# Lower parts of the first layer's weight units: computed by VectorE one pipeline step behind the casts, in place of GpSimd at once

## The chip, the cores and the metric

The kernel runs on one core of a Trainium2 chip, in one launch. The metric is the device time of that launch in microseconds. The engines have a program each and run it in order; they meet by semaphores. PE is TensorE, ACT is ScalarE, DVE is VectorE, POOL is GpSimd, and SP is the engine whose queue issues most DMAs.

## The reference

Retention (attention without softmax, with a decay per head), and then two feed-forward layers. 2304 tokens, 512 wide; the first layer is 2048 wide, the second 1536.

```python
# q, k, v: 4 batches, 8 heads, 576 positions, 64 wide
scores = scale * np.matmul(q, k.transpose(0, 1, 3, 2))
x = np.matmul(scores * Dmat, v)          # Dmat: gamma[h] ** (i - j) for i >= j
x = x.transpose(0, 2, 1, 3).reshape(2304, 512)
h = x @ w_in
x = (h * np.tanh(softplus(h))) @ w_out   # first layer
g = x @ w_gate
out = (silu(g) * (x @ w_val)) @ w_out2   # second layer
```

The weights arrive as 64-bit floats. They are loaded as pairs of 32-bit words and turned into 32-bit floats on the chip.

## The kernel before

**Products in two parts.** Where a product is to have the accuracy of 32-bit floats, each operand is kept as an upper part (the value, cast to the type float32r) and a lower part (the value less the upper part). Three matmuls stand for one product: upper by upper, upper by lower, lower by upper. `prod` (line 511, matmul in line 517) does this for the first product h, and `g2` (line 551) for the second, acc. Of each three matmuls, the second or third reads the lower part of the weights.

**Weight units.** The first layer's weights are cut into 32 units of 128 x 512, in the order in which they are used: `in0` to `in3`, then `in4`, `out0`, `in5`, `out1` and so on to `in15`, `out11`, then `out12` to `out15` (line 67). A unit goes through these steps, each for the unit whose turn it is:

1. `fetch` (line 91): SP loads the raw 64-bit words into one of 4 buffers `raw`. It does nothing while 4 units lie between the unit it would load and the count `stage[3]`.
2. `rebias_raw`: ACT scales the high words (line 103), DVE shifts the low ones (line 104).
3. `sign` (line 108) and `join` (line 112), on DVE: these make the 32-bit float in place.
4. `part`: ACT casts the upper part into the tile u (line 122), and POOL subtracts it from the value for the lower part (line 123). The raw buffer is free when line 123 is done.

The generator `weights` advances this pipeline by one step, for several units at once: signs one, rebiases another, joins the first, casts what is joined, and fetches. With `late` set, the cast is of the unit that an earlier call joined.

**Stages.** Retention comes first, in 20 steps t (line 493). Each step multiplies scores s, transposes the next k (tk), adds to the state, calls `run(weights(NA))`, and forms the output o. DVE masks the scores (p, line 385) and scales the output into x (line 456). ACT copies kT, qT and sbd. POOL scales v (vs, line 364) for the next step. The loads of q, k and v stand on SP's queue among the raw loads, in program order (lines 507 and 508).

Then come 96 slots, `slot(s)` (line 577), with 16 slots (F1) to each of 6 blocks b of 384 tokens. A slot computes h of slot s on PE, then the second product of slot s - 4, then `mish` (ACT, line 568), `halves` (ACT line 573, DVE line 574), and advances the weights: first a loop that runs the pipeline as long as too few units are done, then one call with `late`. Slot 15 does no weights. In their place it splits chunks 2 and 3 of the next block's x into upper parts (ACT, line 252) and lower parts (DVE, line 257). These are `xs_2` and `xs_3`, which h of slot 16 reads in its matmuls 7 to 12. Slots 0 and 1 lie inside retention's last steps.

The engines keep the order in which the program is written. h of slot s reads unit in s for s up to 15, and the second product of slot s - 4 reads unit out s - 4.

Of the kernel before, what the change touches and what calls it, by code (L numbers as in the profile page):

```python
# [7 lines left out]
F32 = mybir.dt.float32  # L8
# [3 lines left out]
ALU = mybir.AluOpType  # L12
# [4 lines left out]
def retention_mish_swiglu(  # L17
# [17 lines left out]
    nc = tc.nc  # L35
    B, H, S, D = q.shape
    NT, DM = out.shape
    F1 = w1_in.shape[1] // 128
# [9 lines left out]
    OFF = 4  # L48
# [18 lines left out]
    todo = []  # L67
# [5 lines left out]
    n1 = len(todo)  # L73
    unit = {}
    pools = {"a": wa}
    raw = {}
    stage = [0, 0, 0, 0]

    def words(j):
        w = raw[j].rearrange("p (n t) -> p n t", t=2)  # L80
        return w[:, :, 0], w[:, :, 1]

    def fetch(lim):
        j = stage[0]
        if j >= min(lim, len(todo)) or j - stage[3] >= RAW:
            return
        stage[0] += 1
        kind, i, src = todo[j]
        raw[j] = xp.tile([128, 2 * DM], U32, tag="raw", name=f"raw{j}", bufs=RAW)
        dst = raw[j] if kind in ("out", "fin") else raw[j].rearrange("p (k f) -> p k f", k=KT)  # L90
        nc.sync.dma_start(out=dst, in_=src)  # L91


    def rebias():
        j = stage[1]
        if j >= stage[0]:
            return
        stage[1] += 1
        rebias_raw(j)
# [6 lines left out]
    def sign(j):  # L106
        lo, hi = words(j)
        nc.vector.scalar_tensor_tensor(lo, hi, 0x80000000, lo, op0=ALU.bitwise_and, op1=ALU.bitwise_or)

    def join(j):  # L110
        lo, hi = words(j)
        nc.vector.scalar_tensor_tensor(lo, hi, 3, lo, op0=ALU.logical_shift_left, op1=ALU.bitwise_or)  # L112

    def part(lim):
        j = stage[3]
        if j >= min(lim, stage[2]):
            return
        stage[3] += 1
        kind, i, _ = todo[j]
        u = pools["a" if j < NA else "b"].tile([128, 2, DM], F32R, tag="u", name=f"u{j}")  # L120
        w = words(j)[0].bitcast(F32)
        nc.scalar.copy(out=u[:, 0, :], in_=w)  # L122
        nc.gpsimd.tensor_tensor(out=u[:, 1, :], in0=w, in1=u[:, 0, :].bitcast(F32), op=ALU.subtract)  # L123
        unit[kind, i] = u


    seen = [0, 0]
# [1 line left out]
    def weights(lim, late=False):  # L129
        j = stage[2]  # L130
        on = j < min(lim, stage[1])
        if on:
            sign(j)
        yield
        if late:
            part(lim)
        if stage[1] < seen[0]:
            rebias()
        seen[:] = seen[1], stage[0]
        yield  # L140
        if on:
            join(j)
            stage[2] += 1
        while not late and stage[3] < stage[2]:
            part(lim)
        fetch(lim + 3)
        seen[1] = stage[0]

    def run(step):
        for _ in step:  # L150
            pass
# [78 lines left out]
    def second(s):  # L230
        if s not in free:
            return
        now = []
        for n in range(2 * PAIRS):
            t = free.index(s) - 5 * n
            if 0 <= t < 5:
                now.append((t, group, (n // 2, n % 2, t)))
            if 4 <= t < 8:
                now.append((t - 4, last, (n, t - 4)))
        for _, f, a in sorted(now, key=lambda x: x[0]):  # L240
            f(*a)
# [8 lines left out]
    def split_hi(d, nm, j, kk):  # L250
        s = xsp.tile([128, 2, T], F32R, tag="xs", name=f"{nm}s{j}_{kk}")
        nc.scalar.copy(out=s[:, 0, :], in_=d[j][:, kk, :])
        xs[nm, j, kk] = s

    def split_lo(d, nm, j, kk, eng):
        s = xs[nm, j, kk]
        eng.tensor_tensor(out=s[:, 1, :], in0=d[j][:, kk, :], in1=s[:, 0, :].bitcast(F32), op=ALU.subtract)
# [10 lines left out]
    nsc = -(-S // 128)  # L268

    def retention(slot):  # L270
        with ExitStack() as c0:
            cp = c0.enter_context(tc.tile_pool(name="cp", bufs=1))
# [220 lines left out]
            for t in range(len(steps)):  # L493
                scores(t)
                transposes(t + 1)
                q_ahead(t, 0)
                state(t)
                q_ahead(t, 1)
                run(weights(NA))
                if t + 1 < nsc:  # L500
                    gout_chunk(t + 1)
                if t == len(steps) - 1:
                    slot(1)
                output(t)
                if t == len(steps) - 3:
                    slot(0)
                load_q(t + 4)
                load(t + 3)

    with tc.manual_schedule():  # L510
# [29 lines left out]
        def g1(s):  # L540
            b, i = divmod(s, F1)
            hs[s] = bank(f"h{s}")
            prod(hs[s], unit["in", i], "x", b)

        def g2(s):
            b, i = divmod(s, F1)
            if i == 0:
                accs[b] = [pools["acc"].tile([128, 512], F32, tag="acc", name=f"acc{b}_{d}") for d in range(KT)]
            u, g = unit["out", i], gs.pop(s)
            for d, a, e, c in order(KT, i == F1 - 1):  # L550
                nc.tensor.matmul(  # L551
                    accs[b][d][:, :T], lhsT=u[:, a, d * 128:(d + 1) * 128], rhs=g[:, e, :],
                    start=(i == 0 and c == 0), stop=(i == F1 - 1 and c == 2),
                )

        def g2_out(s):
            b, i = divmod(s, F1)
            if i == F1 - 1:
                new_x(x2t, b, "y")
                for d in range(KT):  # L560
                    (nc.scalar.copy if d % 2 == 0 else nc.vector.tensor_copy)(  # L561
                        out=x2t[b][:, d, :], in_=accs[b][d][:, :T]
                    )


        def mish(s):
            w = gp.tile([128, T], F32, tag="w", name=f"m{s}")
            nc.scalar.activation(w, hs.pop(s), AF.Mish)  # L568
            ws[s] = w

        def halves(x, s):
            g = gp.tile([128, 2, T], F32R, tag="g", name=f"g{s}", bufs=LAG + 1)
            nc.scalar.copy(out=g[:, 0, :], in_=x)  # L573
            nc.vector.tensor_tensor(out=g[:, 1, :], in0=x, in1=g[:, 0, :].bitcast(F32), op=ALU.subtract)  # L574
            gs[s] = g

        def slot(s):
            b, i = divmod(s, F1)
            if i == 0 and s:
                g2(s - LAG)  # L580
            g1(s)
            if s >= LAG and i:
                g2(s - LAG)
            d, nm, j = xt, "x", b + 1
            parts = () if b + 1 == NB else (i - F1 + 4,) if b and F1 - 4 <= i < F1 - 2 else range(2, KT) if i == F1 - 1 else ()
            mish(s)
            for kk in parts:
                split_hi(d, nm, j, kk)
            halves(ws.pop(s), s)
            if s < F1 + OFF:  # L590
                while not parts and stage[3] < min(2 * s - OFF + 2 if s > OFF else s, n1):
                    run(weights(n1))
            for kk in parts:
                split_lo(d, nm, j, kk, nc.vector)
            if s >= LAG:
                g2_out(s - LAG)
            if s < F1 + OFF and not parts:
                run(weights(n1, True))
            second(s)
# [213 lines left out]
        for u in range(NS2):  # L813
            i = u % PAIRS
# [69 lines left out]
```

## Time and profile before

| | |
|---|---|
| Median of 3 runs | 932.25 us (931.43 to 933.28) |
| The profiled execution | 934.33 us |
| its span, first to last instruction | 932.5 us |
| PE matmuls busy | 912.3 us, 98% |
| VectorE busy | 520.2 us, 56% |
| ScalarE (ACT) busy | 362.3 us, 39% |
| GpSimd (POOL) busy | 108.6 us, 12% |
| L123 on GpSimd, all 32 | 47.1 us, 1473 ns each |
| L122, the casts before it, all 32 | 21.2 us, 663 ns each |

"Busy" is the time in which at least one instruction of the engine ran. A row such as `PE tk L360 <- DMA k: 7.4, 7, 2.0` says that PE stood idle ahead of instructions of line 360 for 7.4 us in all, 7 times, the longest 2.0 us, until a k had landed. In a timeline a row has the start, the length, the engine and the line; `x12` means 12 alike in one row, and brackets give the idle time before it and what ended it. Names have their buffer numbers cut off.

### The profile page before, as it was taken

Reading aid. Unit: us, or ns where it says so; the run is one execution under the profiler, and the core shown is the slowest. Engines: PE = TensorE matmul, PEld = TensorE weight load, DVE = VectorE, ACT = ScalarE, POOL = GpSimd, SP = SyncE. Lnnn points to the kernel's source line nnn. Section 1 sums busy time; section 2 is a strip of 40 time slices with the busy share of each in tenths; the row PEclk is TensorE's granted clock in tenths of the full one; section 3 lists DMA queues with packets and bytes.
Section 4 is the critical chain, followed back from the end, with each engine's and each line's share of the span. In section 5 each row is a group of like instructions: output and inputs, shape, how many; then the busy total and the mean of one; then the engine's idle time right before and its main releaser. Section 6 shows DMA issues by size and latency. Waiting matters only on the chain.

```text
span 932.5 us, 14692 instructions
## 1 busy us (share of the span) xinstructions
PE 912.3 (98%) x5684; PEld 867.8 (93%) x5684; DVE 520.2 (56%) x929; ACT 362.3 (39%) x731; POOL 108.6 (12%) x90
## 2 busy tenths in 40 slices
PE   8888999999999999999999999999999999999998
PEld 7777899999999999999999999998999998999997
DVE  3897797246556565656535444556544556544444
ACT  4776564345444554545434222223222223222222
POOL 3775344000000000000000000000000000000000
PEclk9999999999999999999999999999999999999999
DMA  9999554035354463554554855544644444644421
GB/s 227 249 236 258 146 152 132 1 113 192 127 185 143 142 201 117 166 182 138 175 180 176 296 203 203 203 158 158 226 158 158 158 158 158 226 158 158 158 69 68
DMA packets 115351, 156.58 MB, mean 168 GB/s; under 512 B 45393, under 2 KB 80977, under 8 KB 115281
## 3 DMA queue, kind: packets, MB, share of 16 engines
q1 hardware_dynamic: 114176, 155.21, 53.4%
q8 instruction: 45, 0.74, 0.4%
q10 hardware_dynamic: 1104, 0.42, 0.2%
q14 instruction: 26, 0.20, 0.1%
HBM read 122.58 MB, written 33.03 MB: 167 GB/s over the span
## 4 chain that ended last, share of the span: by engine, by line
PE 88%; DMA 5%; DVE 3%; ACT 2%; SPq 1%; issue 1%; POOL 0%; ACTq 0%; DVEq 0%; POOLq 0%
PE t L777 28%; PE acc L551 20%; PE h L517 20%; PE fa L703 16%; DMA k<-in_k_dram 4%; PE o L436 1%; PE o L443 1%; DMA rawg<-in_moe_w_gate_dram 1%; PE tk L360 1%; PE s L376 1%; PE state L412 0%; DMA comb<-c 0%; DMA q<-in_q_dram 0%; SPq L91 0%; DVE p L385 0%
## 5 line engine op out<-in xcount | busy, mean ns | idle before, releaser
L777 PE MATMUL t<-y,su 128*128 128x384 f32 x1512 | 306.5, 338 | 1.0 <-DVE cv L744 1.0
L777 PEld LDWEIGHTS t<-y,su 128*128 128x128 f32 x1512 | 271.4, 188 | 24.4 <-DVE cv L744 2.3
L551 PE MATMUL acc<-g,u 128*128 128x384 f32 x1152 | 214.6, 336 | 0.9 <-ACT y L561 0.9
L517 PE MATMUL h<-xs,u 128*128 128x384 f32 x1152 | 214.6, 336 | 0.0
L551 PEld LDWEIGHTS acc<-g,u 128*128 128x128 f32 x1152 | 201.3, 188 | 1.5 <-ACT y L561 1.2
L517 PEld LDWEIGHTS h<-xs,u 128*128 128x128 f32 x1152 | 200.9, 188 | 0.3 <-issue 0.2
L703 PE MATMUL fa<-fu,g 128*128 128x512 f32 x648 | 190.0, 395 | 0.1
L703 PEld LDWEIGHTS fa<-fu,g 128*128 128x128 f32 x648 | 118.6, 188 | 7.5 <-ACT g L725 0.5
L574 DVE TENSOR_TENSOR g<-m,g 128x384 fp32r<-128x384 f32 x96 | 53.6, 558 | 126.8 <-ACT g L573 126.4
L725 ACT CAST g<-sg 128x384 fp32r<-128x384 f32 x72 | 36.9, 513 | 175.0 <-DVE sg L762 121.4
L568 ACT ACTIVATE m<-h 128x384 f32<-128x384 f32 x96 | 47.0, 490 | 145.4 <-PE h L517 144.3
L751 ACT ACTIVATE sg<-sg 128x384 f32<-128x384 f32 x54 | 28.4, 525 | 96.4 <-DVE sg L744 96.4
L730 DVE TENSOR_TENSOR g<-sg,g 128x384 fp32r<-128x384 f32 x72 | 40.2, 558 | 40.6 <-ACT g L725 40.6
L177 POOL TENSOR_TENSOR f<-rawf,f 128x256 fp32r<-128x256 f32 x24 | 23.4, 992 | 284.3 <-ACT f L176 284.3
L123 POOL TENSOR_TENSOR u<-raw,u 128x512 fp32r<-128x512 f32 x32 | 47.1, 1473 | 62.7 <-ACT u L122 61.4
L573 ACT CAST g<-m 128x384 fp32r<-128x384 f32 x96 | 49.3, 514 | 2.6
L744 DVE TENSOR_TENSOR u<-t,p 128x384 f32<-128x384 f32 x36 | 20.1, 557 | 49.8 <-PE t L777 45.6
L744 DVE TENSOR_TENSOR v<-t,p 128x384 f32<-128x384 f32 x36 | 20.0, 556 | 38.1 <-PE t L777 37.4
L104 DVE TENSOR_SCALAR raw<-raw 128x512 uint32<-128x512 uint32 x32 | 36.7, 1146 | 0.0
L762 DVE TENSOR_TENSOR sg<-sg,cv 128x384 f32<-128x384 f32 x54 | 30.2, 559 | 1.9
L122 ACT CAST u<-raw 128x512 fp32r<-128x512 f32 x32 | 21.2, 663 | 20.7 <-DVE raw L112 20.7
L364 POOL TENSOR_TENSOR vs<-v,gv 128x512 f32<-128x512 f32 (+1 forms) x20 | 26.3, 1313 | 22.5 <-DMA v<-in_v_dram 13.2
(79 smaller groups left out, 742.7 us busy)
## 6 DMA issues: line engine op xcount, KB each, us to landing
su<-comb SPq DMA_DIRECT2D x126, 512.0 KB, 3.3
comb<-c SPq DMA_DIRECT2D x84, 256.0 KB, 4.0
raw<-in_moe_w_in_dram SPq DMA_DIRECT2D x16, 512.0 KB, 5.8
raw<-in_moe_w_out_dram SPq DMA_DIRECT2D x16, 512.0 KB, 3.7
rawg<-in_moe_w_gate_dram SPq DMA_DIRECT2D x12, 512.0 KB, 6.5
rawf<-in_moe_w_out_dram SPq DMA_DIRECT2D x12, 512.0 KB, 4.5
rawv<-in_moe_w_val_dram SPq DMA_DIRECT2D x12, 512.0 KB, 6.2
find<-f SPq DMA_DIRECT2D x24, 256.0 KB, 2.4
```

Of the source, the lines that this page charges most:

```text
L104: nc.vector.tensor_scalar(lo, lo, 29, None, op0=ALU.logical_shift_right)
L123: nc.gpsimd.tensor_tensor(out=u[:, 1, :], in0=w, in1=u[:, 0, :].bitcast(F32), op=ALU.subtract)
L517: nc.tensor.matmul(ps, lhsT=u[:, a, kk * 128:(kk + 1) * 128], rhs=s[:, e, :], start=(c == 0), stop=(c == n - 1),)
L551: nc.tensor.matmul(accs[b][d][:, :T], lhsT=u[:, a, d * 128:(d + 1) * 128], rhs=g[:, e, :], start=(i == 0 and c == 0), stop=(i == F1 - 1 an ...
L568: nc.scalar.activation(w, hs.pop(s), AF.Mish)
L573: nc.scalar.copy(out=g[:, 0, :], in_=x)
L574: nc.vector.tensor_tensor(out=g[:, 1, :], in0=x, in1=g[:, 0, :].bitcast(F32), op=ALU.subtract)
L703: nc.tensor.matmul(accs["f", b][m], lhsT=gs[u, e, h][:, x, m * 128:(m + 1) * 128], rhs=fu[2 * (u % PAIRS) + e][:, a, :], start=first, stop ...
L725: nc.scalar.copy(out=gs[u, e, h][:, 0, :], in_=x)
L730: nc.vector.tensor_tensor(out=g[:, 1, :], in0=x, in1=g[:, 0, :].bitcast(F32), op=ALU.subtract)
L744: nc.vector.tensor_tensor(out=out_, in0=a, in1=b_, op=ALU.add)
L777: nc.tensor.matmul(p, lhsT=w[:, n % 2, a, kk * 128:(kk + 1) * 128], rhs=y[:, x, kk, :], start=begin and kk == 0 and (a, x) == (0, 0), stop ...
```

## The change

`part` now only casts on ACT and puts the tile on a list, `cast`. A new function `rest` subtracts, on VectorE, for every tile on that list, and it is called at the start of the next `weights` step, ahead of `sign`. The count that `fetch` looks at, `stage[3]`, now counts subtractions done, while `stage[4]` counts casts. The loop in `slot` has a new bound: 2s units (30 in slot 14, where s is F1 - 2) in place of 2s - 2.

```diff
--- before.py
+++ after.py
@@ -74,7 +74,8 @@
     unit = {}
     pools = {"a": wa}
     raw = {}
-    stage = [0, 0, 0, 0]
+    stage = [0, 0, 0, 0, 0]
+    cast = []
 
     def words(j):
         w = raw[j].rearrange("p (n t) -> p n t", t=2)
@@ -112,16 +113,21 @@
         nc.vector.scalar_tensor_tensor(lo, hi, 3, lo, op0=ALU.logical_shift_left, op1=ALU.bitwise_or)
 
     def part(lim):
-        j = stage[3]
+        j = stage[4]
         if j >= min(lim, stage[2]):
             return
-        stage[3] += 1
-        kind, i, _ = todo[j]
+        stage[4] += 1
         u = pools["a" if j < NA else "b"].tile([128, 2, DM], F32R, tag="u", name=f"u{j}")
-        w = words(j)[0].bitcast(F32)
-        nc.scalar.copy(out=u[:, 0, :], in_=w)
-        nc.gpsimd.tensor_tensor(out=u[:, 1, :], in0=w, in1=u[:, 0, :].bitcast(F32), op=ALU.subtract)
-        unit[kind, i] = u
+        nc.scalar.copy(out=u[:, 0, :], in_=words(j)[0].bitcast(F32))
+        cast.append((j, u))
+
+    def rest():
+        while cast:
+            j, u = cast.pop(0)
+            w = words(j)[0].bitcast(F32)
+            nc.vector.tensor_tensor(out=u[:, 1, :], in0=w, in1=u[:, 0, :].bitcast(F32), op=ALU.subtract)
+            unit[todo[j][:2]] = u
+            stage[3] += 1
 
 
     seen = [0, 0]
@@ -129,6 +135,7 @@
     def weights(lim, late=False):
         j = stage[2]
         on = j < min(lim, stage[1])
+        rest()
         if on:
             sign(j)
         yield
@@ -141,7 +148,7 @@
         if on:
             join(j)
             stage[2] += 1
-        while not late and stage[3] < stage[2]:
+        while not late and stage[4] < stage[2]:
             part(lim)
         fetch(lim + 3)
         seen[1] = stage[0]
@@ -588,7 +595,7 @@
                 split_hi(d, nm, j, kk)
             halves(ws.pop(s), s)
             if s < F1 + OFF:
-                while not parts and stage[3] < min(2 * s - OFF + 2 if s > OFF else s, n1):
+                while not parts and stage[3] < min(2 * s + 2 * (s == F1 - 2), n1):
                     run(weights(n1))
             for kk in parts:
                 split_lo(d, nm, j, kk, nc.vector)
```


The lines of the changed kernel are a few higher: 103, 104, 108, 112, 122, 123 become 104, 105, 109, 113, 121, 128; 252, 257, 385, 456, 573, 574 become 259, 264, 392, 463, 580, 581. In the rows below, u, raw, g, m, xs and p are tiles, with the program's numbers behind them.

On PE and SP nothing changes place. First, VectorE in a retention step (t = 8), before:

```order
L385 TENSOR_TENSOR p_8_765<-s_8_755,mask 128x512
L385 TENSOR_TENSOR p_8_766<-s_8_756,mask 128x512
L108 SCALAR_TENSOR_TENSOR raw_591<-raw_591 128x512
L104 TENSOR_SCALAR raw_656<-raw_656 128x512
L112 SCALAR_TENSOR_TENSOR raw_591<-raw_591 128x512
```

and now:

```order
L392 TENSOR_TENSOR p_8_764<-s_8_754,mask 128x512
L392 TENSOR_TENSOR p_8_765<-s_8_755,mask 128x512
L128 TENSOR_TENSOR u_730<-raw_523,u_730 128x512
L109 SCALAR_TENSOR_TENSOR raw_590<-raw_590 128x512
L105 TENSOR_SCALAR raw_655<-raw_655 128x512
L113 SCALAR_TENSOR_TENSOR raw_590<-raw_590 128x512
```

The subtraction of the unit that was cast one step earlier stands between the masks p and the next sign (line 109). This is so in steps 4 to 17. On GpSimd the line 123 that stood between two of line 364 is gone.

Second, VectorE at the end of slot 14 and the start of slot 15, before (g_2045 is slot 14's lower half, g_2084 slot 15's):

```order
L574 TENSOR_TENSOR g_2045<-m_2043,g_2045 128x384
L108 SCALAR_TENSOR_TENSOR raw_1942<-raw_1942 128x512
L112 SCALAR_TENSOR_TENSOR raw_1942<-raw_1942 128x512
L574 TENSOR_TENSOR g_2084<-m_2078,g_2084 128x384
L257 TENSOR_TENSOR xs_2_2080<-x_479,xs_2_2080 128x384
L257 TENSOR_TENSOR xs_3_2082<-x_479,xs_3_2082 128x384
```

and now, from the first subtraction of slot 14 on (g_2082 is slot 15's lower half; u_2029, u_2031, u_2039 and u_2046 are out11, out12, out13 and out14):

```order
L128 TENSOR_TENSOR u_2029<-raw_1882,u_2029 128x512
L128 TENSOR_TENSOR u_2031<-raw_1919,u_2031 128x512
L109 SCALAR_TENSOR_TENSOR raw_1956<-raw_1956 128x512
L105 TENSOR_SCALAR raw_1993<-raw_1993 128x512
L113 SCALAR_TENSOR_TENSOR raw_1956<-raw_1956 128x512
L128 TENSOR_TENSOR u_2039<-raw_1956,u_2039 128x512
L109 SCALAR_TENSOR_TENSOR raw_1993<-raw_1993 128x512
L113 SCALAR_TENSOR_TENSOR raw_1993<-raw_1993 128x512
L128 TENSOR_TENSOR u_2046<-raw_1993,u_2046 128x512
L105 TENSOR_SCALAR raw_2041<-raw_2041 128x512
L581 TENSOR_TENSOR g_2082<-m_2076,g_2082 128x384
L264 TENSOR_TENSOR xs_2_2078<-x_478,xs_2_2078 128x384
```

Where slot 14 had two instructions of weights on VectorE (the last unit's), it now has four subtractions and the signs, joins and shifts of three units, and all of them stand ahead of slot 15's g and xs_2. Ahead of the rows shown come g_2022 (slot 14's lower half) and lines 109, 105 and 113 for out12, out13 and out12.

Third, ACT in the same place, before, from slot 14's upper half g_2045:

```order
L573 CAST g_2045<-m_2043 128x384
L122 CAST u_2049<-raw_1903 128x512
L568 ACTIVATE m_2078<-h_2053 128x384
L252 CAST xs_2_2080<-x_479 128x384
L252 CAST xs_3_2082<-x_479 128x384
L573 CAST g_2084<-m_2078 128x384
```

and now, from slot 14's upper half g_2022:

```order
L580 CAST g_2022<-m_2020 128x384
L104 ACTIVATE raw_1956<-raw_1956 128x512
L121 CAST u_2029<-raw_1882 128x512
L121 CAST u_2031<-raw_1919 128x512
L104 ACTIVATE raw_1993<-raw_1993 128x512
L121 CAST u_2039<-raw_1956 128x512
L121 CAST u_2046<-raw_1993 128x512
L104 ACTIVATE raw_2041<-raw_2041 128x512
L575 ACTIVATE m_2076<-h_2051 128x384
L259 CAST xs_2_2078<-x_478 128x384
L259 CAST xs_3_2080<-x_478 128x384
```

Three more casts of units, and three rebias steps (line 104), now stand between slot 14's upper half and slot 15's mish (m_2076), with the casts of xs_2 and xs_3 behind that.

Between them, slots 2 to 13 now pass four units in five slots, where one passed in each.

## Rows read from the trace of the kernel before

**Rows 1.** Windows: busy us (x count) by engine, granted clock, DMA share, GB/s

```profile
core 0: us, PE busy (x) PEld busy (x) DVE busy (x) ACT busy (x) POOL busy (x), PEclk, DMA share, GB/s
20.00:111.50 91.50, 80.75 (x1073) 69.52 (x1069) 77.10 (x111) 61.12 (x117) 56.12 (x42) 1.00 0.96 229
111.50:174.20 62.70, 62.70 (x363) 62.70 (x362) 46.93 (x63) 34.04 (x64) 23.81 (x15) 1.00 0.38 118
```

**Rows 2.** Waits of PE, 20 to 111.5 us: us in total, times, longest

```profile
PE tk L360 <- DMA k<-in_k_dram: 7.4, 7, 2.0
PE state L412 <- ACT sbd L426: 1.7, 2, 1.1
PE o L443 <- DVE p L385: 1.4, 4, 0.8
```

**Rows 3.** Waits of SP's DMA queue, 20 to 111.5 us

```profile
SPq L91 <- POOL u L123: 23.8, 10, 5.8
```

**Rows 4.** Groups by line, 20 to 111.5 us: count, busy us, mean ns, idle before

```profile
L123 POOL TENSOR_TENSOR u<-raw,u 128x512 fp32r<-128x512 f32 x17 | 23.3, 1371 | 24.3 <-ACT u L122 22.9 <-PE state L412 1.3
L364 POOL TENSOR_TENSOR vs<-v,gv 128x512 f32<-128x512 f32 (+1 forms) x17 | 23.1, 1361 | 10.4 <-PE tk L360 4.4 <-DMA v<-in_v_dram 3.3 <-DMA raw<-in_moe_w_in_dram 2.6
...
L104 DVE TENSOR_SCALAR raw<-raw 128x512 uint32<-128x512 uint32 x19 | 17.8, 935 | 0.0
L108 DVE SCALAR_TENSOR_TENSOR raw<-raw 128x512 uint32<-128x512 uint32 x18 | 17.4, 967 | 0.0
...
L112 DVE SCALAR_TENSOR_TENSOR raw<-raw 128x512 uint32<-128x512 uint32 x17 | 14.9, 878 | 0.0
```

**Rows 5.** Timeline of VectorE with GpSimd idle: start us, length us, instruction

```profile
115.31 0.41 DVE L104 TENSOR_SCALAR raw<-raw 128x512 uint32<-128x512 uint32 x1
115.64 0.68 DVE L112 SCALAR_TENSOR_TENSOR raw<-raw 128x512 uint32<-128x512 uint32 x1
```

**Rows 6.** Timeline of VectorE, slots 13 to 15

```profile
157.65 1.53 DVE L104 TENSOR_SCALAR raw<-raw 128x512 uint32<-128x512 uint32 x1
...
160.73 0.56 DVE L574 TENSOR_TENSOR g<-m,g 128x384 fp32r<-128x384 f32 x1 [0.95 <-ACT g L573]
161.21 0.69 DVE L108 SCALAR_TENSOR_TENSOR raw<-raw 128x512 uint32<-128x512 uint32 x1
161.93 1.68 DVE L112 SCALAR_TENSOR_TENSOR raw<-raw 128x512 uint32<-128x512 uint32 x1
...
166.05 1.02 DVE L257 TENSOR_TENSOR xs<-x,xs 128x384 fp32r<-128x384 f32 x2
```

**Rows 7.** Timelines of GpSimd and VectorE: first and last full retention step with L123

```profile
31.73 1.29 POOL L123 TENSOR_TENSOR u<-raw,u 128x512 fp32r<-128x512 f32 x1
...
31.95 1.68 DVE L108 SCALAR_TENSOR_TENSOR raw<-raw 128x512 uint32<-128x512 uint32 x1
...
94.34 1.29 POOL L123 TENSOR_TENSOR u<-raw,u 128x512 fp32r<-128x512 f32 x1 [1.66 <-ACT u L122]
...
96.15 0.68 DVE L108 SCALAR_TENSOR_TENSOR raw<-raw 128x512 uint32<-128x512 uint32 x1
```

**Rows 8.** Timeline of PE, slots 15 and 16

```profile
161.54 2.24 PE L517 MATMUL h<-xs,u 128*128 128x384 f32 x12
163.62 4.33 PE L551 MATMUL acc<-g,u 128*128 128x384 f32 x24
167.79 4.33 PE L517 MATMUL h<-xs,u 128*128 128x384 f32 x24
```

**Rows 9.** Timeline of ACT, slots 13 and 15

```profile
156.44 0.66 ACT L122 CAST u<-raw 128x512 fp32r<-128x512 f32 x1
157.01 0.71 ACT L103 ACTIVATE raw<-raw 128x512 f32<-128x512 f32 x1
...
163.82 0.49 ACT L568 ACTIVATE m<-h 128x384 f32<-128x384 f32 x1 [2.56 <-PE h L517]
164.21 0.92 ACT L252 CAST xs<-x 128x384 fp32r<-128x384 f32 x2
```

**Rows 10.** Line 91 (raw loads), 134 to 152 us, its last line

```profile
DMA to landing us min/median/max: 3.4/3.5/3.9
```

## The prediction

> **What bounds the kernel now.** I read the windows first. From 111.5 to 174.2 us the matmul row is busy for 62.70 of 62.70 us, at a granted clock of 1.00, which is the 2.4 GHz level; from 20 to 111.5 us, the retention stage, it is busy for 80.75 of 91.50 us [rows 1]. So only retention has PE time to win. In the first layer's slots a faster VectorE buys nothing; a late operand there is lost in full, because nothing downstream stands still to absorb it.
>
> The waits of PE in retention come next: 7.4 us in 7 waits for k landing, 1.7 us for ACT's sbd copies and 1.4 us for VectorE's masked scores p [rows 2]. The k loads stand on SP's queue behind the loads of raw weights, and these wait for L123 on GpSimd, which frees a raw buffer: 23.8 us in 10 waits [rows 3]. Then the groups by line: 17 L123 took 1371 ns each there, while VectorE's L104, L108 and L112 averaged 935, 967 and 878 ns [rows 4]. With GpSimd idle L104 takes 0.41 and L112 0.68 us [rows 5]. So GpSimd and VectorE hold each other up.
>
> **The change part by part.**
>
> *The subtraction itself.* 32 of them leave GpSimd and enter VectorE. No row has this operation on VectorE. The same form over 384 columns (L574) takes 0.56 us, and L108 over 512 columns with two SBUF inputs takes 0.69 [rows 6]; I take 0.69, as the column count is the same, which takes 0.60 of the engine, since a start follows the last one by its length less 0.08 or 0.09 (L108 at 161.21 after L574 at 160.73) [rows 6]. In retention that is 17 x 0.60 = 10.2 us more on VectorE. Against it stand the blocked times: 19 x (935 - 415) + 18 x (967 - 687) + 17 x (878 - 680) ns = 9.9 + 5.0 + 3.4 = 18.3 us [rows 4 to 6]. GpSimd has 23.3 us of L123 beside 23.1 us of L364 [rows 4], so I give half of it, 9.2 us, to L123. VectorE's load in retention then changes by +1.0 us out of 77: nothing.
>
> *When raw buffers come free.* Before, L123 ended on GpSimd at 31.73 + 1.29 = 33.02 us; on VectorE it stands where L108 now starts, 31.95, and ends at 32.64, which is 0.38 earlier. For the last full step it is 95.63 against 96.15 + 0.69 = 96.84, 1.21 later [rows 7]. Over the 14 steps between, worked out in the same way, it goes from 1.1 earlier to 1.7 later, 0.47 later in the mean. On GpSimd L364 moves up past the L123 ahead of it; PE has no wait for L364 in its list [rows 2], so that wins nothing. SP's order is the same, row for row, so each such delay is passed to the raw load and to the k and v behind it. Bounds for retention as a whole: +7 x 0.47 = +3.3 us if every k wait grows by that; -3.1 us if the 1.7 + 1.4 us of waits for ACT and VectorE go [rows 2]. The terms pull against each other and VectorE's sum is zero, so I take 0.
>
> *The slots up to 13.* L104 took 1.53 us there beside L123 and falls to 0.41 [rows 5, 6], which pays for the new 0.69. `fetch` now counts the subtractions done and not the casts issued, so four units pass in five slots where one passed in each. That costs nothing by itself: the first unit that PE could miss is out11, whose lower part is ready at 163.44 (next paragraph), while the product on it starts at 163.62 and needs that part one matmul later [rows 8].
>
> *Slot 14.* What was not done by then is now run at once: the new bound of the loop is 30 units, so the slot takes out11 to out14 in one go, on VectorE and ACT in turns, ahead of slot 15's mish and of the split of x's chunks 2 and 3. Before, these were through early: mish of slot 15 started at 163.82, L252 at 164.21 and L257 at 166.05 [rows 6, 9]; h16, which reads these chunks from its 7th and 8th matmul on, started at 167.79, so its 8th came at 167.79 + 7 x 2.08/12 = 169.00 [rows 8]. That is 2.4 us of slack after 166.05 + 0.55. Now I put the measured durations on the new order, starting from L574 of slot 14 at 160.73 (it hangs on h14 and stays). Starts follow one another as said:
>
> L108(out12) 161.21; L104(out13) 161.81; L112(out12) 162.14, ends 162.82. ACT casts out12 162.86 to 163.52. VectorE subtracts out11 162.75 to 163.44 and out12 163.56. L108(out13) 164.16, L104(out14) 164.76, L112(out13) 165.09 to 165.77. Cast out13 165.81 to 166.47, subtract 166.51, L108(out14) 167.11, L112(out14) 167.83 (0.72 after L108 where nothing stands between, as at 161.93) to 168.51. Cast out14 168.55, then L103(out15) 0.57 later at 169.12, and mish of slot 15 0.62 behind that, at 169.74 [rows 5, 6, 9]. The load of out15 is issued after 163.44 and lands 3.5 us later, 167.0 [rows 10], so it holds nothing up. From mish to L257 it was 166.05 - 163.82 = 2.23 us, so L257 on chunk 2 runs 171.97 to 172.52 [rows 6, 9].
>
> PE's 8th matmul of h16 therefore waits from 169.00 to 172.5: **3.5 us**. Its 7th already waits for L252 (169.74 + 0.39 + 0.5 = 170.6, against 168.83), so it is two gaps of about 1.8 us. PE had no idle time before or behind [rows 1], so all of it reaches the end. With ACT at 0.65 in place of 0.66 and VectorE's starts 0.05 closer or wider, some 14 links give 3.5 +/- 0.7.
>
> The profiled execution took 934.33 us, its span 932.5, against a median of 932.25: 2.1 us more than the median. On the profiled one the sum is 934.33 + 0 + 3.5 = 937.8; on the median 932.25 + 3.5 = **935.75 us**.
>
> **The rivals.**
>
> *A, retention gives it back.* VectorE is freed enough that PE's 3.1 us of waits for ACT and VectorE go: 932.25 + 3.5 - 3.1 = 932.65 us. For it: VectorE was busy for 77.10 of the 91.50 us, and blocked in part of them [rows 1, 4]. Against it: the new work takes as much as the blocking did, and it stands ahead of the next L108.
>
> *B, faster.* The holding-up goes entirely, since the L364 that remain fall beside p, which reads PSUM: then VectorE gains 18.3 - 10.2 = 8 us in retention, L123 ends ahead of where GpSimd ended it, and the k waits shrink too. With 3.1 us and half of the 7.4 [rows 2]: 932.25 + 3.5 - 6.8 = 928.95 us. It decides the sign only if retention wins over 5.4 us. Against it: L364 takes as much of GpSimd as L123 did [rows 4].
>
> L104 at 1.53 us in the slots and at 0.41 alone [rows 5, 6] shows one engine waiting for the other to end. The Trainium skill's page "SBUF — State Buffer", section "Who interferes with whom", gives a rule for this: the two engines share a pair of ports that one instruction keeps to its end, and a VectorE operation with two SBUF inputs contends with a GpSimd one that reads SBUF. The new L123 is such an operation, and L364 such a one, so by the rule L123 would itself be held in retention, and rival C's 939.05 would be the time where the rows alone give 935.75. No row of this trace has that pair.
>
>
> *C, slower twice.* Each L123 on VectorE is late by 0.47 us or more, being held by L364 besides, and each k wait grows by it: 932.25 + 3.5 + 3.3 = 939.05 us.
>
> *D, no stall.* The chain in slot 14 would have to be shorter by 3.5 us. The order of the built kernel has it link by link, so I give this no case of its own; it is in A's chance.
>
> **How the numbers follow.** Forecast 0.52, own range 934.0 to 937.5. A 0.21, B 0.10, C 0.17. This kernel's measurement tells about 0.2%, 1.9 us, from no change: faster means below 930.4, slower above 934.1. The forecast (but for its lowest edge) and C are slower: 0.68. A is the same, with that edge: 0.22. B is faster: 0.10. The range, from A's 932.65 less 0.5 to just under C's 939.05, is 932.1 to 938.8.
>
> **What would show it.** In the profile after: no L123 on GpSimd; L104 near 0.42 us in slots 2 to 13; PE waiting at h16's chunk 2 for ACT and then VectorE, together near 3.5 us, and nowhere else between 111 and 174 us; h0 and h2 within 3 us of where they started. It is wrong if PE passes h16 without a wait, if retention moves by over 3 us, or if the granted clock falls after the gap. The longest wait so far, 2.0 us [rows 2], went by at 1.00.

## The result: 940.57 us, a clear loss and more of it than forecast

| | before | after |
|---|---|---|
| Median | 932.82 us (5 runs, 931.43 to 933.28) | 940.57 us (5 runs, 936.97 to 941.38) |
| The profiled execution, its span | 934.33, 932.5 us | 940.57, 938.8 us |
| VectorE, GpSimd busy | 520.2, 108.6 us | 519.3, 60.7 us |

The ratio is 1.0070, 95% interval 1.0053 to 1.0087. The sign is as predicted. The time lies 4.8 us above the predicted 935.75 and 1.8 us above the range. Of the 4.8 us, 0.57 are the base: the prediction started from 932.25, the median of the kernel before beside this result is 932.82. The rest is a loss of 7.75 us where 3.5 were forecast. Line numbers are up to 7 higher after: L517 is now L524, L551 L558, L252 L259, L257 L264, L364 L371, L360 L367, and L104, L108 and L112 are L105, L109 and L113. The subtraction is L128. A run whose edit adds lines shifts them once more.

First the two stretches of [rows 1], in the profile after:

```profile
20.00:111.50 91.50, 81.29 (x1062) 70.32 (x1060) 81.16 (x129) 60.90 (x117) 31.73 (x25) 0.98 0.96 224
111.50:174.20 62.70, 59.63 (x351) 58.99 (x350) 39.17 (x72) 31.46 (x59) 0.00 (x0) 0.98 0.40 126
```

The columns are as in [rows 1]. GpSimd has lost its work and VectorE is 4.1 us busier in retention. In the second stretch PE, which had no gap before, stands idle for 3.1 us. The granted clock is 0.98 in both. PE around slot 16 answers [rows 8]:

```profile
168.27 1.21 PE L524 MATMUL h<-xs,u 128*128 128x384 f32 x6
171.10 0.44 PE L524 MATMUL h<-xs,u 128*128 128x384 f32 x1 [1.63 <-ACT xs L259]
172.99 5.81 PE L524 MATMUL h<-xs,u 128*128 128x384 f32 x17 [1.45 <-DVE xs L264]
178.59 2.46 PE L558 MATMUL acc<-g,u 128*128 128x384 f32 x12
180.89 2.25 PE L524 MATMUL h<-xs,u 128*128 128x384 f32 x12
```

Here are the two gaps of the forecast: six matmuls of h16, a wait for ACT's half of xs, one matmul, a wait for VectorE's half. The 8th matmul starts at 172.99, where 168.27 + 7 x 2.08/12 = 169.48 would be undelayed: 3.51 us late. But the 17 matmuls behind it take 5.60 us to the next group, not 17 x 0.174 = 2.95. The windows there, with the columns of [rows 1], say why:

```profile
166.00:172.00 6.00, 3.91 (x21) 3.35 (x20) 3.40 (x7) 3.46 (x7) 0.00 (x0) 1.00 0.70 242
172.00:176.00 4.00, 3.02 (x9) 3.02 (x10) 1.40 (x3) 0.98 (x2) 0.00 (x0) 0.52 0.02 4
176.00:180.00 4.00, 4.00 (x16) 4.00 (x16) 2.64 (x5) 1.69 (x4) 0.00 (x0) 0.63 0.00 0
180.00:184.00 4.00, 4.00 (x24) 4.00 (x24) 0.46 (x1) 0.79 (x2) 0.00 (x0) 1.00 0.00 0
```

The granted clock fell inside the second gap to 0.5, the 1.2 GHz level, and PE worked at that level until 179.0 us. In windows of 1 us it is 0.57 at 172 to 173, 0.50 from 173 to 178, 0.52 at 178 to 179, and 1.00 behind. From the start of h16 to the start of h17 it is 180.89 - 168.27 = 12.62 us, against 174.06 before - 167.79 [rows 8] = 6.27.

Now the chain in slot 14 which makes xs late, VectorE first and ACT second, to hold against the forecast's link by link and [rows 6, 9]:

```profile
163.23 1.52 DVE L128 TENSOR_TENSOR u<-raw,u 128x512 fp32r<-128x512 f32 x2
...
167.00 0.69 DVE L128 TENSOR_TENSOR u<-raw,u 128x512 fp32r<-128x512 f32 x1 [0.72 <-ACT u L121]
...
169.74 0.69 DVE L128 TENSOR_TENSOR u<-raw,u 128x512 fp32r<-128x512 f32 x1 [0.71 <-ACT u L121]
...
172.38 1.02 DVE L264 TENSOR_TENSOR xs<-x,xs 128x384 fp32r<-128x384 f32 x2
```

```profile
166.32 0.65 ACT L121 CAST u<-raw 128x512 fp32r<-128x512 f32 x1 [1.73 <-DVE raw L113]
169.06 0.65 ACT L121 CAST u<-raw 128x512 fp32r<-128x512 f32 x1 [2.09 <-DVE raw L113]
...
170.18 0.47 ACT L575 ACTIVATE m<-h 128x384 f32<-128x384 f32 x1
170.55 0.91 ACT L259 CAST xs<-x 128x384 fp32r<-128x384 f32 x2
```

Each engine waits for the other in turn; one round, from cast to cast, is 169.06 - 166.32 = 2.74 us. The mish of slot 15 stands behind the last cast and one rebias. All of it is 0.4 to 0.5 us later than forecast, because h2 started at 111.97 us and not at 111.47.

### The profile page after: what moved, and what is told of

Its sections match the earlier page's. It is cut to its first block, busy times and chain, and to the rows that moved or that the text cites. A ratio compares the mean times of both kernels' runs of the same rounds, so it can differ in the third digit from the quotient of the medians.

```text
span 938.8 us, 14594 instructions
## 1 busy us (share of the span) xinstructions
PE 916.3 (98%) x5684; PEld 871.5 (93%) x5684; DVE 519.3 (55%) x961; ACT 362.3 (39%) x731; POOL 60.7 (6%) x58
## 4 chain that ended last, share of the span: by engine, by line
PE 87%; DMA 6%; DVE 4%; ACT 2%; SPq 1%; issue 1%; POOL 0%; ACTq 0%; DVEq 0%; POOLq 0%
PE t L784 28%; PE h L524 20%; PE acc L558 20%; PE fa L710 16%; DMA k<-in_k_dram 3%; PE o L450 1%; PE o L443 1%; DMA rawg<-in_moe_w_gate_dram 1%; DVE p L392 1%; DMA v<-in_v_dram 1%; DVE u L128 1%; DMA q<-in_q_dram 0%; DMA comb<-c 0%; PE s L383 0%; DVE raw L109 0%
## 5 line engine op out<-in xcount | busy, mean ns | idle before, releaser
L524 PE MATMUL h<-xs,u 128*128 128x384 f32 x1152 | 217.7, 339 | 3.1 <-ACT xs L259 1.6
L558 PE MATMUL acc<-g,u 128*128 128x384 f32 x1152 | 214.8, 336 | 0.3 <-ACT y L568 0.3
L524 PEld LDWEIGHTS h<-xs,u 128*128 128x128 f32 x1152 | 203.3, 190 | 3.9 <-ACT xs L259 1.9
L558 PEld LDWEIGHTS acc<-g,u 128*128 128x128 f32 x1152 | 201.6, 188 | 1.0 <-ACT y L568 0.7
L371 POOL TENSOR_TENSOR vs<-v,gv 128x512 f32<-128x512 f32 (+1 forms) x20 | 24.2, 1208 | 57.4 <-DMA v<-in_v_dram 46.5
L109 DVE SCALAR_TENSOR_TENSOR raw<-raw 128x512 uint32<-128x512 uint32 x32 | 26.1, 815 | 0.0
L392 DVE TENSOR_TENSOR p<-s,mask 128x512 f32<-128x512 f32 (+1 forms) x40 | 23.5, 627 | 3.9 <-PE s L383 3.6
```

Of the source, the lines that this page charges most:

```text
L392: nc.vector.tensor_tensor(out=pp[t][e][:n, :, :n], in0=s[e][:n, :, :n], in1=mask[:n, :n].unsqueeze(1).to_broadcast([n, NP, n]), op=ALU.mult,)
L524: nc.tensor.matmul(ps, lhsT=u[:, a, kk * 128:(kk + 1) * 128], rhs=s[:, e, :], start=(c == 0), stop=(c == n - 1),)
L558: nc.tensor.matmul(accs[b][d][:, :T], lhsT=u[:, a, d * 128:(d + 1) * 128], rhs=g[:, e, :], start=(i == 0 and c == 0), stop=(i == F1 - 1 an ...
```

## Experiments

The question was what of the loss is the wait, what is the clock, and what is retention. "Before" is the median of the kernel before on the same chip.

**e1: the same change with no bundle in slot 14.**

```diff
             if s < F1 + OFF and not parts:
-                run(weights(n1, True))
+                for _ in range(1 + (s in (3, 5, 8, 10, 13))):
+                    run(weights(n1, True))
```

> The changed kernel, but with one more step of the weight units at the end of slots 3, 5, 8, 10 and 13, so that slot 14 starts with 31 of the 32 units finished and has no step to pass ahead of slot 15's mish and splits. Theory (the loss is the PE wait behind slot 14's four steps, and the fall of the granted clock that follows it): h16 is passed without a wait, PEclk is 1.00 from 160 to 184 us, and what is left is the retention's part, +0.4 us at the start of h2: 933.3 us (932.3 to 934.3), ratio 1.0005. Rival (the subtraction on VectorE costs time wherever it stands, since VectorE's load rises): the 14 units behind retention still cost, 936 us or more. Second rival (steps packed into earlier slots stall PE there): a wait of 0.5 us or more on a mish, a split or a u in slots 4 to 14.

Measured: 933.37 us, before 933.61, ratio 1.0000 (0.9989 to 1.0010). PE has no wait between 111.5 and 185 us, the clock is 1.00 there, and h16 to h17 takes 6.27 us, as before:

```profile
168.71 4.33 PE L524 MATMUL h<-xs,u 128*128 128x384 f32 x24
...
174.98 2.25 PE L524 MATMUL h<-xs,u 128*128 128x384 f32 x12
```

So the 15 subtractions that VectorE does behind retention cost nothing within 0.9 us; when they run decides. Retention in this profile was 0.9 us longer than in the one before (h2 at 112.41), and its granted clock dropped too (0.79 at 34 to 42 us); over twelve executions the time doesn't show it.

**e2: one step fewer in slot 14.**

```diff
-                while not parts and stage[3] < min(2 * s + 2 * (s == F1 - 2), n1):
+                while not parts and stage[3] < min(2 * s, n1):
```

> The changed kernel, with the extra 2 in slot 14's bound taken out (28 in place of 30): the slot runs two steps and the late one, where it ran three and the late one, and so has one cast and one subtraction less on the chain. By the rows of the changed kernel ScalarE is then free for mish 15 at 167.0 in place of 170.18, its splits end at 168.3, VectorE's join ends at 169.0, g's half at 169.5 and the first lower half of xs at 170.0, needed at 169.6: a PE wait of 0.4 us (0 to 1.0) in place of 3.1 in two gaps. Theory of stall and clock: no fall of PEclk, 933.7 us (933.0 to 934.8). Rival (the clock falls for the load of VectorE or for the earlier part of the kernel, not for the wait): PEclk falls below 0.7 at 172 us all the same, 936.5.

Measured: 935.41 us, before 933.61, ratio 1.0024 (1.0013 to 1.0035). The wait came as worked out:

```profile
169.38 1.38 PE L524 MATMUL h<-xs,u 128*128 128x384 f32 x7
171.12 3.27 PE L524 MATMUL h<-xs,u 128*128 128x384 f32 x17 [0.35 <-DVE xs L264]
```

The clock stayed at 1.00, and h16 to h17 took 6.96 us, 0.69 more than undisturbed. So leaving out one round between the two engines took away nearly the whole of the wait. The time missed its expectation by 1.7 us: ratio and wait leave some 1.5 us over (0.0024 x 933.6 = 2.2, less 0.69). The mean granted clock over its executions was 0.997 where before had 0.998, and h2 started at 113.09 us in its profile, with the retention code of e1. That remainder isn't explained.

**e3 and e9: one half of the change each.** In e3 retention subtracts on GpSimd as before, the slots as after; e9 is the reverse, with the bound of before. The edit for e3 (the pool `"b"` is opened when retention has ended, so the test means "in retention"; e9 tests `"b" in pools`):

```diff
         nc.scalar.copy(out=u[:, 0, :], in_=w)
+        if "b" not in pools:
+            nc.gpsimd.tensor_tensor(out=u[:, 1, :], in0=w, in1=u[:, 0, :].bitcast(F32), op=ALU.subtract)
+            unit[todo[j][:2]] = u
+            stage[3] += 1
+            return
         cast.append((j, u))
```

> One part of the change alone: in retention the subtraction is GpSimd's at once, as before; behind retention it is VectorE's, one step behind, with the changed bound. Theory: the start of h2 is back at 111.5 us, the wait at h16 is there with 3.5 us in two gaps, the clock falls behind it, 940.1 us (938 to 941). Rival (the retention part is the loss, its clock dip at 53 us included): 935 us or less.

> The other part of the change alone: in retention the subtraction is VectorE's, one step behind; behind retention it is GpSimd's at once, with the bound of before. Theory: no wait at h16, the clock 1.00 from 112 to 400 us, and retention within 0.5 us of before's on average: 933.6 us (932.6 to 934.8), ratio 1.000. Rival (the retention part costs by VectorE's 4 us of extra load): 935.5 us or more.

e3: 933.01 us, before 933.61, ratio 0.9996 (0.9984 to 1.0008). My expectation fell: there was no wait at h16. Its ACT rows show why:

```profile
161.38 0.65 ACT L122 CAST u<-raw 128x512 fp32r<-128x512 f32 x1
164.04 0.68 ACT L122 CAST u<-raw 128x512 fp32r<-128x512 f32 x1 [2.00 <-DVE raw L113]
...
166.24 0.70 ACT L104 ACTIVATE raw<-raw 128x512 f32<-128x512 f32 x1 [0.95 <-DMA raw<-in_moe_w_out_dram]
166.81 0.50 ACT L581 ACTIVATE m<-h 128x384 f32<-128x384 f32 x1
```

There are two casts in slot 14 in place of four, and mish starts at 166.81, not 170.18. By the program, GpSimd leaves no unit cast but not yet subtracted at retention's end; by ACT's rows the slots without a cast are then others, and two casts are left for slot 14. The stall needs both halves of the change: the slots' part with its new bound, and the lag that retention hands on.

e9: 934.71 us, before 933.30, ratio 1.0011 (0.9998 to 1.0024), no wait at h16. By this half and e1, VectorE's part in retention costs between nothing and 2 us; the two intervals don't settle more.

**e4: work put where PE waited.** In h16's product, 10 matmuls without use (L525 in its rows) stand ahead of the 7th and 9 ahead of the 8th, into the bank that h17 takes next.

```diff
                 for a, e in ((0, 0), (0, 1), (1, 0)):
+                    for _ in range({6: 10, 7: 9}.get(c, 0) if fill is not None else 0):
+                        nc.tensor.matmul(fill, lhsT=u[:, 0, :128], rhs=xs[nm, j, 0][:, 0, :], start=True, stop=True)
```

> The changed kernel with 19 matmuls without use put in h16's product, 10 ahead of its 7th matmul and 9 ahead of its 8th, written to the bank that h17 takes next: TensorE works where it waited, and what it waits for comes no sooner. Theory (the clock falls because TensorE stood idle): the 8th real matmul starts at about 173.0 as in the changed kernel, PEclk stays at 1.00 from 172 to 180, the 17 matmuls that follow take 2.95 us in place of 5.60, and the time is 2.8 us under the changed kernel's: 936.8 us (935.8 to 938.3). Rival (the clock falls for another reason): PEclk 0.5 to 0.6 at 172 to 178 and 939.5 to 940.6 us.

```profile
167.92 1.21 PE L526 MATMUL h<-xs,u 128*128 128x384 f32 x6
168.97 1.90 PE L525 MATMUL h<-xs,u 128*128 128x384 f32 x10
170.75 0.44 PE L526 MATMUL h<-xs,u 128*128 128x384 f32 x1
171.03 1.72 PE L525 MATMUL h<-xs,u 128*128 128x384 f32 x9
172.64 3.24 PE L526 MATMUL h<-xs,u 128*128 128x384 f32 x17
175.72 2.27 PE L563 MATMUL acc<-g,u 128*128 128x384 f32 x12
177.83 2.25 PE L526 MATMUL h<-xs,u 128*128 128x384 f32 x12
```

The useful 8th matmul (L526) comes as late as in the changed kernel, 172.64 - 169.13 = 3.51 us, yet the 17 behind it take 3.08 us and the clock is 1.00 from 166 to 184. h16 to h17 is 167.92 to 177.83, 9.91 us: 3.64 for the wait alone. Median 938.20 us, before 933.61, ratio 1.0051 (1.0032 to 1.0070). The changed kernel did not run beside it, so the comparison was made again on one chip (e13 to e16).

**e5 to e7 and e13 to e16: both gaps, one, or none.** e5 and e13 are the changed kernel; e6 and e15 fill the first gap only (`{6: 10}`), e7 and e16 the second only (`{7: 9}`), e14 is e4 again.

> The changed kernel itself once more, on the chip of the runs below. Theory: the two gaps at h16 again (1.6 and 1.45 us, 8th matmul 3.5 us late), the clock down behind them; in 20 to 60 us a fall of the clock may or may not be there, as among the kernels so far; 938.5 to 941 us.

> The changed kernel with 10 matmuls without use ahead of h16's 7th alone: the first gap is filled, the second of 1.45 us stays. If it is the two gaps together that bring the clock down: PEclk 1.00 in 172 to 180 us, 937.5 us (936.5 to 939). If a gap of 1.4 us is enough by itself: PEclk 0.5 to 0.6 there and 940 us. So far one wait of 1.60 to 1.68 us at the eighth tk step was followed by a fall, and waits of 1.80, 1.96 and 2.03 us elsewhere were not; I lean to no fall, 0.6.

> The changed kernel with 9 matmuls without use ahead of h16's 8th alone: the second gap is filled, the first of 1.63 us stays. As for the other half: no fall and 937.5 us if it takes both gaps (0.6), a fall and 940 us if 1.63 us is enough (0.4).

> The changed kernel, in five rounds, beside the three filled versions on the same chip. Theory: mean granted clock 0.9955 against 0.998 of the kernel before, since the clock falls behind h16's gaps in most executions; 939.3 us (938.5 to 940.5).

> Both gaps of h16 filled with matmuls without use. Theory: the stall stays, the fall at h16 doesn't come; 2.0 us (1.2 to 2.8) under the changed kernel, mean granted clock higher by 0.002. Rival (the fall comes as often in either, or in neither): within 0.7 us of it.

> The first gap of h16 filled, the second of 1.45 us left. If a fall needs both gaps: as with both filled, within 0.6 us. If one gap will do: between the two, or as the changed kernel.

> The second gap of h16 filled, the first of 1.63 us left. If a fall needs both gaps: as with both filled, within 0.6 us. If one gap will do: between the two, or as the changed kernel.

| | left to PE | median us | ratio, interval | h16 to h17 in the profile |
|---|---|---|---|---|
| e5 | both gaps | 938.98 | 1.0063 (1.0048 to 1.0078) | 9.91, clock 1.00 |
| e13 | both gaps | 940.16 | 1.0075 (1.0059 to 1.0092) | 12.55, clock falls |
| e15 | second | 937.91 | 1.0045 (1.0031 to 1.0059) | 9.91, clock 1.00 |
| e16 | first | 938.08 | 1.0049 (1.0033 to 1.0065) | 9.91, clock 1.00 |
| e14 | none | 937.20 | 1.0048 (1.0030 to 1.0065) | 9.90, clock 1.00 |
| e6 | second | 938.80 | 1.0055 (1.0039 to 1.0072) | 9.89, clock 1.00 |
| e7 | first | 937.92 | 1.0043 (1.0027 to 1.0060) | 9.94, clock 1.00 |

e13 to e16 shared a chip (before 933.62), as did e5 to e7 (before 933.19). Windows of e13, then of e14, columns as in [rows 1]:

```profile
172.00:176.00 4.00, 3.15 (x10) 3.15 (x11) 1.34 (x4) 1.00 (x2) 0.00 (x0) 0.50 0.02 4
176.00:180.00 4.00, 4.00 (x18) 4.00 (x17) 2.70 (x5) 1.67 (x3) 0.00 (x0) 0.65 0.00 0
```

```profile
172.00:176.00 4.00, 4.00 (x24) 3.79 (x23) 2.16 (x5) 1.00 (x2) 0.00 (x0) 1.00 0.02 4
176.00:180.00 4.00, 4.00 (x25) 4.00 (x24) 2.25 (x4) 1.56 (x3) 0.00 (x0) 1.00 0.00 0
```

The wait is the same in all seven: the useful 8th matmul of h16 comes 3.5 us late. Filling any one of the two gaps takes as much off the time as filling both: the mean ratio of e14 to e16 is 1.0047 against e13's 1.0075, a difference of 0.0028 or 2.6 us, what one fall costs in the profiles (12.55 - 9.91 = 2.64). The means of all executions say the same, 940.50 us (6) against 937.92 (22), and the mean granted clock is 0.994 against 0.9965. The intervals of single ratios still overlap, and on the chip of e5 to e7 the difference is half as large and not clear of noise: 939.45 us (4) against 938.15 (6). The profiles agree with one another: with a gap filled the clock stayed up at h16 in 6 of 6, with both left it fell in 3 of 4 (after, e8 and e13, not e5). So at h16 the fall came only with both gaps close together, and then most of the time. What spared e5 isn't settled.

**e8: one more step in slot 14** (`3 * (s == F1 - 2)` in the bound).

> The changed kernel with 3 in place of 2 added to slot 14's bound: one more step stands ahead of slot 15's mish. By the rows of the changed kernel the chain grows by a rebias, a sign, a join and the cast behind them: mish 15 comes 2.2 us later (172.4 in place of 170.2), and the 8th matmul of h16 with it, 5.7 us late in place of 3.5. Theory (each step in slot 14 is worth its round trip between VectorE and ScalarE): 2.0 to 2.8 us more stall, 941.5 to 944 us with the clock's fall. Rival (the stall is set by something else that comes late, a landing or the ring of xs): stall as before, 939.5 to 940.6.

Measured: 940.83 us, before 933.19, ratio 1.0088 (1.0066 to 1.0110), with the clock's fall. The wait grew by 0.3 us, not by 2.2: the gaps are 1.62 and 1.75 us, the 8th matmul 3.8 us late. Slot 15's mish on ACT, then VectorE:

```profile
170.59 0.47 ACT L575 ACTIVATE m<-h 128x384 f32<-128x384 f32 x1
```

```profile
171.29 0.69 DVE L109 SCALAR_TENSOR_TENSOR raw<-raw 128x512 uint32<-128x512 uint32 x1
172.02 0.69 DVE L113 SCALAR_TENSOR_TENSOR raw<-raw 128x512 uint32<-128x512 uint32 x1
172.63 0.55 DVE L581 TENSOR_TENSOR g<-m,g 128x384 fp32r<-128x384 f32 x1
```

I had put a cast behind the added join, ahead of mish; the step that was added has its cast after mish (at 176.65). What was left to add, a sign and a join, fell beside the time in which VectorE waited for ACT's mish, splits and g anyway. So by e2 and e8 the unit of the stall is a round between the engines, not a step.

**e10: VectorE at once, with no lag**, the kernel before with `nc.vector` in place of `nc.gpsimd` in L123.

> The kernel before with the engine of the subtraction alone changed: VectorE takes it at once, right behind the cast of the same step, with the bound of before. Theory (VectorE works in order and now stands through each cast): some 17 steps of retention have VectorE blocked for 0.7 us more each, 12 us more of VectorE's time, of which 2 to 6 us reach PE, since VectorE had 14 of 91 us free: 935.5 to 939.5 us; behind retention no wait at h16, as no units are bundled in slot 14. Rival (the step of lag buys nothing, since VectorE has room): 933 to 934.5 us.

Measured: 933.52 us, before 933.30, ratio 1.0003 (0.9993 to 1.0013). VectorE stood through the casts as expected, but the 2 to 6 us that I gave for it did not come: the rival held, and it cost nothing. Groups by line of VectorE, 20 to 111.5 us, columns as in [rows 4]:

```profile
L123 DVE TENSOR_TENSOR u<-raw,u 128x512 fp32r<-128x512 f32 x17 | 13.7, 804 | 11.7 <-ACT u L122 11.6
...
L456 DVE TENSOR_TENSOR x<-o,gout 128x512 f32<-128x512 f32 (+1 forms) x20 | 11.6, 590 | 7.1 <-PE o L443 7.1
```

It waited 11.6 us for ACT, but 7.1 us for PE's o where before it was 13.6: idle time that it had in each step moved to another place. The step of lag bought nothing in retention, and behind it the lag and the new bound are what built the bundle.

**e11 and e12: the raw fetch behind the loads of the step.** In retention `weights` no longer fetches; `fetch` follows `load(t + 3)`. e11 is e1 with this, e12 the kernel before with it.

```diff
-                run(weights(NA))
+                run(weights(NA, fill=False))
...
                 load_q(t + 4)
                 load(t + 3)
+                fetch(NA + 3)
+                seen[1] = stage[0]
```

> The spread version with the fetch of the next raw unit put behind the loads of the step in retention, in place of ahead of them: the loads of k no longer stand in SP's queue behind its wait for u. Theory (PE's 6 to 7 us of waits for k come from that queue): PE's waits for k fall below 4 us, retention ends 1 to 4 us earlier, and with fewer waits the clock falls less often: 931 us (929 to 932.8). Rival (the loads then wait for buffers of their own, or the raw units come later and hold up the steps): h2 starts at 112 us or later, 933 to 936 us.

> The kernel before with the same move of the fetch alone. Theory as for the spread version: 931 us (929 to 933); if it gains as much there, the gain has nothing to do with the engine of the subtraction. Rival: no gain, since the loads of k wait for their buffers, 933 to 936 us.

e11: 932.54 us, ratio 0.9989 (0.9980 to 0.9998). e12: 931.26 us, ratio 0.9978 (0.9968 to 0.9988), before 933.30. So e12 beats both kernels: the one before by 2.0 us, the changed one by some 8 to 10 (these 2.0 and its own loss of 5.8 to 7.75). PE's waits in it, 20 to 111.5 us, against [rows 2]:

```profile
PE state L413 <- ACT sbd L427: 3.8, 5, 1.2
PE tk L361 <- DMA k<-in_k_dram: 1.8, 2, 1.5
```

and in e11:

```profile
PE tk L368 <- DMA k<-in_k_dram: 5.2, 6, 1.4
```

In e12 the waits for k went from 7.4 to 1.8 us, and a part came back as waits for ACT's sbd (3.8 against 1.7). The gain needs no change of engine. In e11 the time came within its expectation, but the mechanism did not: the waits for k stayed at 5.2 us, where e1 had 6.7 and I expected less than 4. By the mean ratios the move was worth half as much with VectorE's subtraction (0.0011 from e1 to e11, 0.0022 for e12); the intervals are too wide to say so, and why k still waited isn't settled.

## Why the prediction was right on the wait and wrong on the clock

**The failed step: the clock behind the gap.** The forecast took the granted clock as 1.00 throughout, since the longest wait of the trace, 2.0 us, had gone by at 1.00, and named a fall only among the things that would show it wrong. It fell. In the profile h16 to h17 grew by 6.35 us, of which 3.64 is the wait (e4) and 2.71 the clock. Over the executions of one chip it is 2.6 us (e13 against e14 to e16), over the few of another 1.3 (e5 against e6 and e7). The precedent was poor twice over: it was one gap, where h16 has two with one matmul, 0.44 us, between, and one execution, where the retention of kernels built alike fell in some and not in others. The Trainium skill's page "TensorE: Matmul & The Clock Gate", Part 1, says that the clock is gated by how busy the engine has been of late. The filled runs agree: matmuls without use kept it at 1.00.

**Slot 14: right.** 3.5 us were predicted and 3.51 measured for the 8th matmul, in two gaps (1.63 and 1.45, forecast as about 1.8 each). Order and durations were right link by link: L128 took 0.69 us, as taken from L108. e1 and e2 show the bundle as its cause.

**Slots 2 to 13: right.** No wait of PE; the stall began nowhere else.

**Retention: taken as 0, in fact 0 to 1 us.** h2 started 0.50 us later in the profile. In 13 profiles with VectorE's subtraction one step behind in retention, with the fetch where it was, it started at 111.6 to 115.1 us, 112.8 in the mean; in the two with GpSimd's at 111.47 and 112.25, and in the one with VectorE's at once (e10) at 110.77. The timed runs give 0 (e1, -1.0 to +0.9 us) and +1.0 (e9, -0.2 to +2.2). The 0.8 us that e14 to e16 leave lie between: 0.0047 x 933.6 = 4.4, less 3.64. Part of it may be falls of the granted clock in retention, which the forecast did not weigh either. In the four kernels with VectorE's subtraction in retention and no gap at h16, the mean granted clock lay 0.0006 (e1), 0.0020 (e9), 0.0015 (e10) and 0.0009 (e11) under that of the kernel before beside them; in the two with GpSimd's it lay 0.0007 (e3) and 0.0002 (e12) above. No run separates this from the waits. The load of VectorE was mis-sized: +1.0 us predicted, +4.1 measured. Of the 18.3 us of blocking I gave half to L123; the groups of after, with columns as in [rows 4], still hold 11.3:

```profile
L109 DVE SCALAR_TENSOR_TENSOR raw<-raw 128x512 uint32<-128x512 uint32 x18 | 16.5, 915 | 0.0
L113 DVE SCALAR_TENSOR_TENSOR raw<-raw 128x512 uint32<-128x512 uint32 x18 | 13.9, 773 | 0.0
L105 DVE TENSOR_SCALAR raw<-raw 128x512 uint32<-128x512 uint32 x19 | 13.4, 703 | 0.0
L128 DVE TENSOR_TENSOR u<-raw,u 128x512 fp32r<-128x512 f32 x17 | 12.5, 738 | 0.0
```

That is 19 x (703 - 415) + 18 x (915 - 687) + 18 x (773 - 680) ns = 5.5 + 4.1 + 1.7 us; what was won is 7.0, not 9.2. L128 that were held, the next point, and one L113 more in the window add to it.

**The rivals.** PE's waits in the profile after, against [rows 2]:

```profile
PE tk L367 <- DMA k<-in_k_dram: 5.7, 6, 1.7
PE o L450 <- DVE p L392: 1.6, 2, 1.4
PE state L419 <- ACT sbd L433: 0.9, 1, 0.9
PE state L419 <- POOL vs L371: 0.8, 1, 0.8
PE o L450 <- POOL vs L371: 0.7, 1, 0.7
PE o L443 <- ACT sbd L433: 0.3, 1, 0.3
```

A fails: of the 3.1 us of waits for ACT and VectorE 2.8 stayed, and 1.5 us for GpSimd's vs, which before had none, came in. B fails with it, as retention gained nothing. C named a time near the one measured, 939.05, for a reason that did not act: the waits for k were 5.7 us, not 10.7 (7.3 in e5 and 6.7 in e13, the same kernel). Its cause exists on a small scale. Here VectorE, then GpSimd:

```profile
52.52 1.28 DVE L128 TENSOR_TENSOR u<-raw,u 128x512 fp32r<-128x512 f32 x1
```

```profile
52.22 1.04 POOL L371 TENSOR_TENSOR vs<-v,gv 64x512 f32<-64x512 f32 x1 [1.96 <-DMA v<-in_v_dram]
```

The Trainium skill's rule in "SBUF — State Buffer", "Who interferes with whom", agrees: beside a GpSimd instruction that reads SBUF, L128 took 1.28 us in place of 0.68. In this profile that pair met twice in 17, for 1.0 us in all (1.28 and 1.10 against 0.68). That is the least of the three profiles of this kernel: in e5 six L128 were held for 2.9 us in all, in e13 five for 2.6. D, no stall, fails.

**The sum.** The forecast had 0 + 3.5 + 0. Measured are about 0.8 for retention, 3.64 for the wait and 2.6 for the clock: 7.0 us. That this meets e13 is no check, since the first and the last term come out of the ratios of e13 to e16 (0.0075 x 933.6 = 7.0); the others are: the median differences are 7.75 (after) and 5.8 (e5, where the profile has no fall at h16).

## What to carry to other kernels

A stall of a TensorE that was never idle can have two prices, its own length and what the granted clock takes afterwards; for a gap of a few us forecast both, with a chance on the second (here 3.6 us, and 2.6 in 3 of 4 profiles). When a lag is added to a pipeline, count what is still unfinished at the places where work is forced to the end: the cost stood in one slot where four steps ran in a row, and spreading them over earlier slots took it away. The dear part of this bundle was the number of round trips between two engines (2.74 us each), not the operations in it (0.69).

## What the hardware showed

- Two gaps of 1.6 and 1.4 to 1.8 us with one matmul between brought the granted clock down to 0.5 for some 7 us (172.1 to 179.0 us after), in 3 of 4 profiles; either gap alone did not in 4 of 4. In retention, where PE is idle more often, falls came behind some single waits for k (1.68 us at 51 us after, 2.83 us in e3) and not behind others (1.96 us in e2).
- The kernel before has falls too: its mean granted clock was 0.996 to 1.000 over 35 executions beside e9 to e12, though its profiled one shows 1.00 in every window.
